# Second-weight operands made in the chunk loop, and M1, M6, M7 summed in one PSUM bank

## The chip, the cores and the metric

The kernel runs on one core of one Trainium2 chip. Times are microseconds on the device. The program is short of nothing but order: five engines work side by side, each through its own queue in the order in which the kernel was written down, TensorE (PE) for matmuls, VectorE (DVE) and ScalarE (ACT) for everything that reads PSUM, GpSimd (POOL) for work between SBUF tiles, SyncE (SP) for issuing DMAs.

## The reference

The input x has 2048 tokens of 576 numbers. With xn the layer norm of x:

```
s = linear_attention(xn, wqkv) @ wo        # 32 heads of 18
h = gelu(xn @ w1 + b1)                     # 576 -> 4608, tanh form
g = silu(h @ w2 + b2)                      # 4608 -> 576
out = x + s * g
```

All of it is in float32. A float32 number is split into a high part that TensorE takes in one pass and a low part, the rest; a product is then three matmuls (high by high, high by low, low by high).

## The kernel before, in words

The program has four stages. First, tokens are normalised and transposed and the keys and values projected, 16 tiles of 128 tokens (the loop over `t`, lines 539 to 640). Second, the queries and the attention output (lines 1069 to 1105). Third, the two dense layers, 18 chunks (lines 1511 to 1607). Fourth, the end of the last chunk with the plain second product and the gate (lines 1608 to 1610).

The chunk loop does the work of the two dense layers with a scheme of seven products in place of eight. A half of the chunks (9) treats 1024 tokens, a chunk 4 of the 36 column tiles of w1 (128 columns each). In a chunk there are two `Up` blocks (j = 0 and 1; class at line 1129), each for a pair of column tiles and two blocks of 512 tokens. An `Up` block computes seven products M1 to M7, each of seven matmuls of 512 columns at line 1147, and from them four outputs, which go through GELU on ACT (line 1155). The order of the seven is written out in `UP` (line 1453). Their sums, with U1 and U2 for partial sums, are:

```
g(0,0) = M1 + M2              U1 = M1 + M6        U2 = U1 + M7
g(1,0) = U1 + M5 + M3         g(1,1) = U2 + M5    g(0,1) = U2 + M4
```

After the two blocks come the seven products of the second layer (`product`, line 1273; order in `ORDER`, line 1269), each in two calls of 24 matmuls in all, added to `macc` by DVE (line 1292). Their moving operands come from the blocks B00, B01, B10, B11 of w2, four of them through differences: operand 5 is B01 - B00, operand 7 is B11 - B01, operand 6 is B11 less operand 5, operand 4 is B10 less operand 6. Each operand is split: its high part by ACT (`set_hi`, line 812), its low part by DVE (`set_lo`, line 815). The stationary operands are the GELU outputs and their sums (class `HOps`; POOL makes the sums at lines 1243 to 1252).

Where the operands of w2 come from differs. In the first half a chunk loads the raw block (line 667), and makes operands 2, 1, 7, 4 and 3 itself, with three subtractions on POOL (lines 1200 and 1205); it stores each to DRAM (line 809) for the second half, which only loads. Operands 5 and 6 were made in the projection stage, for all nine chunks (lines 389 to 423), and stored; both halves load them (line 1223). The operands of w1 are made in the first half's chunks too (class `W1`: four subtractions on POOL at lines 858 to 865, splits at 869 and 874).

PSUM has eight banks here: a pool of two one-bank tiles (`bank1`), from which an `Up` block takes A and E, and a pool of three two-bank tiles (`bank2`), from which it takes two, and every second-layer product one.

What sets the order: a chunk has 28 steps, 7 for each `Up` block and 14 for the half products. At each step the code emits the product, then what the tables have put at that step (`at_step`, line 1495): `P1` and `P0` for w1, `PW2` for w2 (the step of each high part; its low part comes one step later), `PH` for the GELU outputs. The engines run all this strictly in the order in which it was emitted (`in_order`, line 1509), each engine for itself. A matmul that writes a bank waits until the engines that read the bank before are done with it.

```
UP = (1, 6, 7, 5, 2, 3, 4)
PW2 = {2: 0, 1: 1, 7: 3, 4: 5, 3: 8}
ORDER = (1, 2, 7, 4, 5, 3, 6)
```

Of the kernel before, what the change touches and what calls it, by code (L numbers as in the profile page):

```python
# [44 lines left out]
def linear_attention_gated_ffn(ctx, tc, x, xT, wqkv, wo, w1, w1e, b1, w2, b2, out):  # L45
# [90 lines left out]
    w2p = ph1.enter_context(tc.tile_pool(name="w2p", bufs=2, reuse_waits="tile"))  # L136
# [252 lines left out]
    T_OPS = (5, 6)  # L389
    w2raw, w2op = {}, {}  # L390

    def w2_load(c):
        t = w2p.tile([P, 3, 2, HD], F32, tag="w2r", name=f"w2r{c}")
        nc.sync.dma_start(t.rearrange("p b a d -> p (b a d)"), w2[c][:, D:])
        w2raw[c] = t

    def w2_block(c, i):

        B11, B00, B01 = (w2raw[c][:, k] for k in range(3))
        return {5: (B00, B01, B00), 6: (B11, B11, B00)}[i]  # L400

    def w2_sum(j):
        c, i = j // 2, T_OPS[j % 2]
        dst, a, b = w2_block(c, i)
        nc.gpsimd.tensor_tensor(dst, a, b, op=SUB)

    def w2_hi(j):
        shape = [P, 2, 2, HD]
        if j % 4 < 2:
            w2op[j] = stw.tile(shape, F32R, tag="stw", name=f"w2o{j}")  # L410
        else:
            w2op[j] = w2p.tile(shape, F32R, tag="w2o", name=f"w2o{j}")
        nc.scalar.copy(w2op[j][:, 0], w2_block(j // 2, T_OPS[j % 2])[0])

    def w2_lo(j):
        c, i = j // 2, T_OPS[j % 2]
        t = w2op[j]
        nc.vector.tensor_tensor(t[:, 1], w2_block(c, i)[0], t[:, 0].bitcast(F32), op=SUB)

    def w2_store(j):  # L420
        c, i = j // 2, T_OPS[j % 2]
        w2_dram[c, i] = d = dram.tile([P, 2, 2, HD], F32, name=f"op_{c}_{i}")
        nc.sync.dma_start(d, w2op.pop(j).bitcast(F32))

# [33 lines left out]
    W2_AT = (2, 4, 6, 8, 10, 11, 12, 13, 14)  # L458
    W2_LOADS = {0: 0, 1: 1, 3: 2, 5: 3, 7: 4, 9: 5, 11: 6, 12: 7, 13: 8}
    W2_SUMS = {t: (2 * c, 2 * c + 1) for c, t in enumerate(W2_AT)}  # L460

    class XSums:
# [19 lines left out]
        def tt(self, out, a, b, op):  # L482
            nc.vector.tensor_tensor(out, a.bitcast(F32), b.bitcast(F32), op=op)
# [24 lines left out]
        def sum4(self, k):  # L508
            self.tt(self.t, (self.h0, self.l0)[k][:, self.B], self.t, (SUB, ADD)[k])
# [29 lines left out]
    for t in range(NT):  # L539
# [21 lines left out]
        sums2 = W2_SUMS.get(t - 1, ())  # L561
# [17 lines left out]
        if t + 1 < NTR:  # L579
            if t:  # L580
                k_t, _ = phi(t1, pk, f"k{t}", values)
            transpose_x(t + 1)
            if t == 0:
                project(t, wv_h, wv_l, pv, FIRST_V[1], cols=v_cols, begin=False)
            for j in sums2:
                w2_hi(j)
            for j in sums2:
                w2_lo(j)
            if t - 1 in WE_SUMS:
                we_hi(WE_SUMS[t - 1]), we_lo(WE_SUMS[t - 1])  # L590
            if t == 0:
                layernorm(2)
            if t + 2 < NTR:
                offset(t + 2)
            if t == 0:
                k_t, _ = phi(t1, pk, f"k{t}")
        else:
            if not last:
                set_x_hi(t + 1), set_x_lo(t + 1)
            for j in sums2:  # L600
                w2_hi(j)
            for j in sums2:
                w2_lo(j)
# [16 lines left out]
        for j in W2_SUMS.get(t, ()):  # L620
            w2_sum(j)
# [6 lines left out]
        for j in W2_SUMS.get(t - 1, ()):  # L628
            w2_store(j)
# [5 lines left out]
        if t in W2_LOADS:  # L635
            w2_load(W2_LOADS[t])
# [490 lines left out]
    m1_sb, u1_sb, u2_sb = (mid[:, i] for i in range(3))  # L1127

    class Up:


        def __init__(self, n, w, xs):
            self.p, self.w = n % NP, w
            self.xb = xs

            self.a, self.b = bank1(f"a{n}"), bank2(f"b{n}")
            self.zy, self.e = bank2(f"zy{n}"), bank1(f"e{n}")
            self.g = {}
# [19 lines left out]
        def step(self, i):  # L1158
            A, B, E = self.a, self.b[:, 0, :], self.e
            Z, Y = self.zy[:, 0, :], self.zy[:, 1, :]  # L1160
            tt = nc.vector.tensor_tensor
            if i == 1:
                self.mm(A, 1)
                nc.scalar.copy(m1_sb, A)  # L1164
            elif i == 6:
                self.mm(B, 6)
                tt(u1_sb, B, m1_sb, op=ADD)  # L1167
            elif i == 7:
                self.mm(Z, 7)
                tt(u2_sb, Z, u1_sb, op=ADD)  # L1170
            elif i == 5:
                self.mm(E, 5)
                tt(B, E, u2_sb, op=ADD)  # L1173
                self.gelu(1, 1, B)
            elif i == 2:
                self.mm(A, 2, first=False)
                self.gelu(0, 0, A)
            elif i == 3:
                self.mm(E, 3, first=False)
                tt(E, E, u1_sb, op=ADD)  # L1180
                self.gelu(1, 0, E)
            else:
                self.mm(Y, 4)
                tt(Y, Y, u2_sb, op=ADD)
                self.gelu(0, 1, Y)


    class W2:
# [5 lines left out]
        def load_raw(self):  # L1194
            self.raw = raw = load_w2_raw(self.n) if self.n else w2_raw0[0]
            self.B = lambda r, n: raw[:, 2 - 2 * r + n]
            self.src = {1: self.B(0, 0), 2: self.B(1, 0), 3: self.B(1, 1), 7: self.B(0, 1)}

        def sum7(self):
            nc.gpsimd.tensor_tensor(self.src[7], self.src[3], self.src[7], op=SUB)  # L1200

        def sum4(self, k):

            self.src[4] = t = self.src[2]
            nc.gpsimd.tensor_tensor(t, t, self.src[(7, 1)[k]], op=SUB)
# [247 lines left out]
    UP = (1, 6, 7, 5, 2, 3, 4)  # L1453
# [21 lines left out]
    PW2 = {2: 0, 1: 1, 7: 3, 4: 5, 3: 8}  # L1475
    W2_SUMS_NEXT = {5: 23, 6: 27}
    W2_SUMS_FIRST = {5: 6, 6: 10}
# [33 lines left out]
    for step in range(n_chunks):  # L1511
# [19 lines left out]
        if half == 0 and c < NC - 1:  # L1531
# [5 lines left out]
            for i, at in W2_SUMS_NEXT.items():  # L1537
                add(base + at, lambda i=i, n=step + 1: w2t[n].load(i))
# [119 lines left out]
```

## Time and profile before

| | before |
|---|---|
| runs, median of 3 (lowest, highest) | 1097.93 us (1097.7, 1102.11) |
| span of the profiled execution, first to last instruction | 1096.2 us |
| TensorE busy | 1088.2 us, 6702 matmuls |
| VectorE, ScalarE, POOL busy | 829.5, 491.3, 471.5 us |
| mean granted TensorE clock | 0.999 |

The profile is of one execution. Its own time on the device is known only as the span; the runs' median is 1.7 us above it. A row of a group reads: line, engine, operation, output and input tile, shape, count; then busy time and mean ns; then the idle time of the engine in front of it and what ended that. A row of the timeline reads: start in us, duration, engine, line, operation, and in brackets the engine's idle time in front of it. A row of stretches reads: the stretch, its length, the busy time of PE, PE's weight loads, DVE, ACT and POOL (with counts), the granted clock, the DMA engines' busy share and GB/s. The chain's rows are start, duration, engine, tile, line.

### The profile page before, as it was taken

Reading aid. Unit: us, or ns where it says so; the run is one execution under the profiler, and the core shown is the slowest. Engines: PE = TensorE matmul, PEld = TensorE weight load, DVE = VectorE, ACT = ScalarE, POOL = GpSimd, SP = SyncE. Lnnn points to the kernel's source line nnn. Section 1 sums busy time; section 2 is a strip of 40 time slices with the busy share of each in tenths; the row PEclk is TensorE's granted clock in tenths of the full one; section 3 lists DMA queues with packets and bytes.
Section 4 is the critical chain, followed back from the end, with each engine's and each line's share of the span. In section 5 each row is a group of like instructions: output and inputs, shape, how many; then the busy total and the mean of one; then the engine's idle time right before and its main releaser. Section 6 shows DMA issues by size and latency. Waiting matters only on the chain.

```text
span 1096.2 us, 18083 instructions
## 1 busy us (share of the span) xinstructions
PE 1088.2 (99%) x6702; PEld 1008.8 (92%) x6702; DVE 829.5 (76%) x1132; ACT 491.3 (45%) x844; POOL 471.5 (43%) x403
## 2 busy tenths in 40 slices
PE   9999999999999999999999999999999999999998
PEld 8999989999898998989989989899898998989987
DVE  7787748888798888888888888667475584764856
ACT  6555555555545455454453544524234243242442
POOL 3676434323546446464554553424234143242340
PEclk9999999999999999999999999999999999999999
DMA  7898834675959558486585769978676676767452
GB/s 248 264 274 274 309 137 149 206 248 186 333 221 350 182 220 322 160 320 224 189 332 175 284 237 400 391 248 289 215 241 219 210 231 212 238 219 224 126 184 87
DMA packets 88400, 262.54 MB, mean 239 GB/s; under 512 B 11894, under 2 KB 24182, under 8 KB 85624
## 3 DMA queue, kind: packets, MB, share of 16 engines
q1 hardware_dynamic: 88312, 261.38, 69.3%
q8 instruction: 53, 0.87, 0.3%
q14 instruction: 35, 0.29, 0.1%
HBM read 164.24 MB, written 95.17 MB: 237 GB/s over the span
## 4 chain that ended last, share of the span: by engine, by line
PE 99%; DVE 1%; ACT 0%; issue 0%; POOL 0%; DVEq 0%; POOLq 0%
PE pm L1286 35%; PE a L1147 10%; PE e L1147 10%; PE zy L1147 10%; PE pk L321 6%; PE pq L321 5%; PE ps_s L788 5%; PE b L1147 5%; PE pv L321 4%; PE pd L1402 2%; PE ps_kva L382 1%; PE ptp L770 1%; PE ps_kw L707 1%; PE warm L369 0%; DVE wkv_l L364 0%; PE ps_kvb L382 0%
## 5 line engine op out<-in xcount | busy, mean ns | idle before, releaser
L1292 DVE TENSOR_TENSOR macc<-pm,macc 128x576 f32<-128x576 f32 x218 | 163.9, 752 | 49.9 <-PE pm L1286 48.4
L812 ACT CAST h_h<-g 128x512 fp32r<-128x512 f32 x204 | 121.9, 621 | 132.7 <-PE pm L1286 131.5
L815 DVE TENSOR_TENSOR h_l<-g,h_h 128x512 fp32r<-128x512 f32 x204 | 161.8, 800 | 0.0
L1252 POOL TENSOR_TENSOR mid<-g 128x512 f32<-128x512 f32 x34 | 43.9, 1292 | 108.1 <-ACT g L1155 108.1
L1246 POOL TENSOR_TENSOR g<-g 128x512 f32<-128x512 f32 x34 | 54.9, 1616 | 49.5 <-DVE h_l L815 28.4
L1155 ACT ACTIVATE g<-b,b1c 128x512 f32<-128x512 f32 x36 | 24.8, 690 | 102.5 <-DVE b L1173 102.5
L1164 ACT COPY mid<-a 128x512 f32<-128x512 f32 x36 | 21.1, 585 | 95.3 <-PE a L1147 95.3
L858 POOL TENSOR_TENSOR w1raw<-w1raw 128x256 f32<-128x256 f32 x18 | 13.3, 737 | 116.8 <-ACT h_h L812 68.2
L1167 DVE TENSOR_TENSOR mid<-b,mid 128x512 f32<-128x512 f32 x36 | 24.8, 690 | 45.0 <-PE b L1147 41.8
L1374 POOL TENSOR_TENSOR fin1l<-fin1h,fin1l 128x288 f32<-128x288 f32 x8 | 6.5, 811 | 118.4 <-DMA fin1l<-s_dram 69.6
L1249 POOL TENSOR_TENSOR g<-g 128x512 f32<-128x512 f32 x34 | 55.2, 1623 | 2.7
L1147 PE MATMUL a<-h0r,wa 128*128 128x512 f32 x144 | 50.4, 390 | 0.0
L1147 PE MATMUL a<-xh,wa 128*128 128x512 f32 x144 | 50.4, 390 | 0.0
L815 DVE TENSOR_TENSOR h_l<-mid,h_h 128x512 fp32r<-128x512 f32 x34 | 48.8, 1436 | 1.2
L1155 ACT ACTIVATE g<-e,b1c 128x512 f32<-128x512 f32 x36 | 24.8, 690 | 51.9 <-DVE e L1180 51.9
L753 POOL TENSOR_TENSOR pbuf<-phiq,den 128x576 f32<-128x576 f32 x16 | 19.4, 1213 | 63.6 <-DVE den L752 63.6
L1243 POOL TENSOR_TENSOR g<-g 128x512 f32<-128x512 f32 x34 | 44.1, 1296 | 2.7
L1180 DVE TENSOR_TENSOR e<-e,mid 128x512 f32<-128x512 f32 x36 | 24.8, 690 | 22.3 <-PE e L1147 22.3
L1170 DVE TENSOR_TENSOR mid<-zy,mid 128x512 f32<-128x512 f32 x36 | 24.9, 691 | 19.8 <-PE zy L1147 19.8
L1173 DVE TENSOR_TENSOR b<-e,mid 128x512 f32<-128x512 f32 x36 | 25.2, 700 | 18.5 <-PE e L1147 17.4
L321 PE MATMUL pk<-wkv_h,xh 128*128 128x288 f32 (+1 forms) x160 | 38.2, 321 | 0.4 <-ACT xh L248 0.4
L321 PE MATMUL pk<-wkv_l,xh 128*128 128x288 f32 (+1 forms) x160 | 38.4, 321 | 0.0
(857 smaller groups left out, 3646.5 us busy)
## 6 DMA issues: line engine op xcount, KB each, us to landing
we<-we_dram SPq DMA_DIRECT2D x36, 448.0 KB
w2raw<-w SPq DMA_DIRECT2D x10, 1152.0 KB
op<-w2o SPq DMA_DIRECT2D x18, 576.0 KB
w1raw<-w SPq DMA_DIRECT2D x18, 512.0 KB
op_a<-wa SPq DMA_DIRECT2D x18, 512.0 KB
op_c<-wc SPq DMA_DIRECT2D x18, 512.0 KB
op_d<-wd SPq DMA_DIRECT2D x18, 512.0 KB
wc<-op_c SPq DMA_DIRECT2D x18, 512.0 KB
```

The costliest lines, as they stand in the source:

```text
L321: nc.tensor.matmul(ps[:, h, : ws.stop - ws.start], st, w[:, k, ws], start=(begin and i == 0), stop=(end and i == len(seq) - 1), skip_group ...
L788: nc.tensor.matmul(ps[:, h, :HD], st[:, k, :], w[:, k, h * HD : (h + 1) * HD], start=(i == 0), stop=(i == len(seq) - 1),)
L812: nc.scalar.copy(pair[0], src)
L815: eng.tensor_tensor(pair[1], src, pair[0].bitcast(F32), op=SUB)
L1147: nc.tensor.matmul(ps, st, mv, start=first and n == 0, stop=n == len(seq) - 1, skip_group_check=True,)
L1155: nc.scalar.activation(g, ps, AF.Gelu_apprx_tanh, bias=b1c[:, f : f + 1])
L1243: tt(src[5, pr], A(1, 0), A(1, 1), op=ADD)
L1246: tt(src[6, pr], src[5, pr], A(0, 0), op=SUB)
L1249: tt(src[3, pr], A(0, 1), src[6, pr], op=SUB)
L1252: tt(src[7, pr], A(0, 0), A(1, 0), op=SUB)
L1286: nc.tensor.matmul(ps[:, q, :HD], hs[p][st][:, cs], m[:, p, :], start=(n == 0 and i not in CHAIN), stop=(n == 5), skip_group_check=True,)
L1292: nc.vector.tensor_tensor(dst, src, dst, op=ADD)
```

## The change

**The projection stage** no longer makes operands 5 and 6 of w2. Nine loads, 18 subtractions on POOL, 18 splits on ACT and on DVE and 18 stores go, with their tables and the pool `w2p`.

**A chunk of the first half** makes operands 5 and 6 itself. In place of three subtractions on POOL (operand 7 in one, operand 4 in two) it does four, in the order 5, 7, 6, 4, at steps 3 and 4, each overwriting a block of the raw tile. The high and low parts of operands 1, 2 and 3 come ahead of them, those of 7, 4, 5, 6 behind. Operands 5 and 6 are stored like the others, and no longer loaded in the first half. The second half's loads are as before.

**An `Up` block** has the order 1, 2, 6, 5, 7, 3, 4. M1, M6 and M7 are accumulated by TensorE in bank A, one after the other; ACT copies the bank to SBUF after each (M1, then U1, then U2). ACT also copies M5 from E, into the place where M1 was. DVE adds four times (M2 + M1, U2 + M5, M3 + U1, M4 + U2) where it added five times. The two-bank tiles are now `bc`, with M2 in one bank and M4 in the other, and `z`, which only DVE writes (U2 + M5).

```diff
-    T_OPS = (5, 6)
...
-        for j in W2_SUMS.get(t, ()):
-            w2_sum(j)
...
+    m5_sb = m1_sb
...
-            self.a, self.b = bank1(f"a{n}"), bank2(f"b{n}")
-            self.zy, self.e = bank2(f"zy{n}"), bank1(f"e{n}")
+            self.a, self.e = bank1(f"a{n}"), bank1(f"e{n}")
+            self.bc, self.z = bank2(f"bc{n}"), bank2(f"z{n}")
...
+            A, E, Z = self.a, self.e, self.z[:, 0, :]
+            B, C = self.bc[:, 0, :], self.bc[:, 1, :]
             if i == 1:
                 self.mm(A, 1)
                 nc.scalar.copy(m1_sb, A)
+            elif i == 2:
+                self.mm(B, 2)
+                tt(B, B, m1_sb, op=ADD)
+                self.gelu(0, 0, B)
             elif i == 6:
-                self.mm(B, 6)
-                tt(u1_sb, B, m1_sb, op=ADD)
-            elif i == 7:
-                self.mm(Z, 7)
-                tt(u2_sb, Z, u1_sb, op=ADD)
+                self.mm(A, 6, first=False)
+                nc.scalar.copy(u1_sb, A)
             elif i == 5:
                 self.mm(E, 5)
-                tt(B, E, u2_sb, op=ADD)
-                self.gelu(1, 1, B)
-            elif i == 2:
-                self.mm(A, 2, first=False)
-                self.gelu(0, 0, A)
-            elif i == 3:
+                nc.scalar.copy(m5_sb, E)
+            elif i == 7:
+                self.mm(A, 7, first=False)
+                tt(Z, A, m5_sb, op=ADD)
+                nc.scalar.copy(u2_sb, A)
+                self.gelu(1, 1, Z)
+            elif i == 4:
+                self.mm(C, 4)
+                tt(C, C, u2_sb, op=ADD)
+                self.gelu(0, 1, C)
+            else:
                 self.mm(E, 3, first=False)
                 tt(E, E, u1_sb, op=ADD)
                 self.gelu(1, 0, E)
-            else:
-                self.mm(Y, 4)
-                tt(Y, Y, u2_sb, op=ADD)
-                self.gelu(0, 1, Y)
...
+        def T(self, i):
+            src = self.src
+            tt = nc.gpsimd.tensor_tensor
+            B00, B01, B10, B11 = (self.B(r, n) for r in range(2) for n in range(2))
+            dst, a, b = {
+                5: (B00, B01, B00), 7: (B01, B11, B01), 6: (B11, B11, B00), 4: (B10, B10, B11)
+            }[i]
+            tt(dst, a, b, op=SUB)
+            src[i] = dst
...
-    UP = (1, 6, 7, 5, 2, 3, 4)
+    UP = (1, 2, 6, 5, 7, 3, 4)
...
-    PW2 = {2: 0, 1: 1, 7: 3, 4: 5, 3: 8}
+    PW2 = dict(
+        T={5: 3, 7: 3, 6: 4, 4: 4},
+        hi={2: 0, 1: 1, 3: 2, 7: 5, 4: 6, 5: 8, 6: 9},
+        lo={2: 1, 1: 2, 3: 3, 7: 6, 4: 7, 5: 9, 6: 10},
+    )
...
-            add(base, w2t[step].sum7)
-            for k in range(2):
-                add(base + 2, w2t[step].sum4, k)
-            for i, at in PW2.items():
-                add(base + at, w2t[step].hi, i)
-                add(base + at + 1, w2t[step].lo, i)
-            if step == 0:
-                for i, at in W2_SUMS_FIRST.items():
-                    add(at, w2t[0].load, i)
+            for what in ("T", "hi", "lo"):
+                for i, at in PW2[what].items():
+                    add(base + at, getattr(w2t[step], what), i)
...
-            for i, at in W2_SUMS_NEXT.items():
-                add(base + at, lambda i=i, n=step + 1: w2t[n].load(i))
```

More of the change, by code (lines that the diff above doesn't have):

```diff
@@ L135, in linear_attention_gated_ffn @@
     stw = ph1.enter_context(tc.tile_pool(name="stw", bufs=2, reuse_waits="tile"))
-    w2p = ph1.enter_context(tc.tile_pool(name="w2p", bufs=2, reuse_waits="tile"))
     t1 = ph1.enter_context(tc.tile_pool(name="t1", bufs=2, side="right", reuse_waits="tile"))
@@ L385, in state @@
             )
-    T_OPS = (5, 6)
[L390 to L410, printed above, removed]
-        else:
[L412 to L423, printed above, removed]
     we = {}
@@ L457, in linear_attention_gated_ffn @@
     WE_SUMS = {2 * q + 1: q for q in range(WG)}
-    W2_AT = (2, 4, 6, 8, 10, 11, 12, 13, 14)
-    W2_LOADS = {0: 0, 1: 1, 3: 2, 5: 3, 7: 4, 9: 5, 11: 6, 12: 7, 13: 8}
-    W2_SUMS = {t: (2 * c, 2 * c + 1) for c, t in enumerate(W2_AT)}
     class XSums:
@@ L560, in linear_attention_gated_ffn @@
         v_t = v_bufs[t % 2]
-        sums2 = W2_SUMS.get(t - 1, ())
         last = t + 1 == NT
@@ L584, in linear_attention_gated_ffn @@
                 project(t, wv_h, wv_l, pv, FIRST_V[1], cols=v_cols, begin=False)
[L585 to L588, printed above, removed]
             if t - 1 in WE_SUMS:
@@ L599, in linear_attention_gated_ffn @@
                 set_x_hi(t + 1), set_x_lo(t + 1)
[L600 to L603, printed above, removed]
             if t - 1 in WE_SUMS:
@@ L627, in linear_attention_gated_ffn @@
             raw_q[k] = load_w_raw(0, k)
-        for j in W2_SUMS.get(t - 1, ()):
-            w2_store(j)
         if t - 1 in WE_SUMS:
@@ L1196, in load_raw @@
             self.B = lambda r, n: raw[:, 2 - 2 * r + n]
[L1197 to L1205, printed above, removed]
+            self.src = {1: self.B(0, 0), 2: self.B(1, 0), 3: self.B(1, 1)}
+        def T(self, i):
[7 more added lines that the diff above has]
+            src[i] = dst
         def plain(self, f):
```

7 lines of the change are left out of this document (removed).

## The prediction

> **What bounds the kernel now.** I read first the page's busy times and its row of granted clock, then a table of stretches, then the chain that ended last.
>
> ```profile
> span 1096.2 us, 18083 instructions
> PE 1088.2 (99%) x6702; PEld 1008.8 (92%) x6702; DVE 829.5 (76%) x1132; ACT 491.3 (45%) x844; POOL 471.5 (43%) x403
> PEclk9999999999999999999999999999999999999999
> ...
> 0.00:20.00 20.00, 17.39 (x104) 16.31 (x105) 13.52 (x30) 12.59 (x22) 6.90 (x17) 1.00 0.92 326
> 40.00:80.00 40.00, 40.00 (x248) 38.79 (x247) 35.58 (x48) 21.99 (x43) 30.34 (x28) 1.00 1.01 288
> 283.00:685.00 402.00, 402.00 (x2393) 366.80 (x2392) 348.74 (x456) 193.75 (x333) 206.33 (x167) 1.00 0.71 263
> 685.00:1087.00 402.00, 402.00 (x2397) 367.19 (x2396) 259.86 (x349) 139.77 (x225) 130.84 (x101) 1.00 0.67 225
> ```
>
> TensorE sets the end: in both halves of the chunk loop it is busy for 402.00 of 402.00 us, at clock 1.00. The change leaves every matmul in place, so it can gain only where TensorE idles or runs slower. It idles 2.6 us of the first 20, before any product of the chunk loop, and in the tail. For pace I compare chunks in the chain:
>
> ```profile
> 551.47 1.62 PE a L1147 x7
> 553.10 1.60 PE b L1147 x7
> 596.19 1.62 PE a L1147 x7
> ...
> 819.63 1.62 PE a L1147 x7
> 864.29 1.62 PE a L1147 x7
> ```
>
> A chunk takes 44.72 us in the first half and 44.66 in the second, although VectorE works 348.74 us in the one and 259.86 in the other. Taking all of that difference away would give 9 x 0.06 = 0.5 us. With the whole 2.6 us at the start the change can gain at most 3.1 us (0.3%). What is left to ask is whether a matmul has to wait in the new order.
>
> **Work that goes away or moves under cover.** These groups price it:
>
> ```profile
> L405 POOL TENSOR_TENSOR w2r<-w2r 128x576 f32<-128x576 f32 x18 | 28.8, 1598 | 15.6 <-DVE phik L340 8.5 <-DMA w2r<-w 6.4
> L413 ACT CAST w2o<-w2r 128x576 fp32r<-128x576 f32 x18 | 11.5, 672 | 2.5 <-POOL w2r L405 2.5
> L418 DVE TENSOR_TENSOR w2o<-w2r,w2o 128x576 fp32r<-128x576 f32 x18 | 19.1, 1098 | 0.2
> L1164 ACT COPY mid<-a 128x512 f32<-128x512 f32 x36 | 21.1, 585 | 95.3 <-PE a L1147 95.3
> L1167 DVE TENSOR_TENSOR mid<-b,mid 128x512 f32<-128x512 f32 x36 | 24.8, 690 | 45.0 <-PE b L1147 41.8 <-ACT mid L1164 3.2
> op<-w2o SPq DMA_DIRECT2D x18, 576.0 KB
> ```
>
> The projection stage loses 28.8 us of POOL, 11.5 of ACT and 19.1 of VectorE with 9 loads and 18 stores; TensorE is full there (40.00 of 40.00), so that is worth 0. In the chunk loop's first half 18 loads of 576 KB turn into 16 stores at a DMA share of 0.71: 0. On SP's queue the two new stores of a chunk wait for low parts that end, in the walk below, at 19.8 and 20.9, and the next chunk's second load of we stands behind them; its first use is after 44.7, so 0 as well. One VectorE addition fewer in each of 36 Up blocks takes 36 x 0.69 = 25 us from VectorE, three more ScalarE copies give ScalarE 36 x 3 x 0.585 = 63 us. Their sums are covered by 44.7 us of matmuls a chunk; what counts is where each stands in its queue.
>
> **The new waits.** Before, M2 went onto bank A four products after M1, and M3 onto E two after M5. Now M6 goes onto A two products after M1, M7 onto A two after M6, M3 onto E two after M5. Each waits until ScalarE has copied the bank, and one product of cover lies between: 1.6 us, as the row of M6 at 553.10 above has it (1.59 from product to product). The copies stand in ScalarE's queue behind the weight splits, and these behind POOL. So I walk the queues of a first-half chunk. Time 0 is its first matmul, at 551.31.
>
> ```profile
> 551.31 0.40 PE L1147 MATMUL a<-xh,wa 128*128 128x512 f32 x1
> 554.27 0.69 DVE L874 TENSOR_TENSOR wa<-w1raw,wa 128x512 fp32r<-128x512 f32 x1 [1.18 <-ACT wa L869]
> 559.87 1.22 DVE L874 TENSOR_TENSOR wc<-w1raw,wc 128x512 fp32r<-128x512 f32 x1 [0.62 <-ACT wc L869]
> 561.01 1.98 DVE L815 TENSOR_TENSOR w__6302<-w2raw,w__6302 128x576 fp32r<-128x576 f32 x1
> 564.91 0.76 DVE L815 TENSOR_TENSOR w__6336<-w2raw,w__6336 128x576 fp32r<-128x576 f32 x1
> 555.04 0.74 POOL L858 TENSOR_TENSOR w1raw<-w1raw 128x256 f32<-128x256 f32 x1 [4.76 <-DVE wa L874]
> 555.86 1.14 POOL L861 TENSOR_TENSOR w1t<-w1raw 128x256 f32<-128x256 f32 x1
> 556.96 1.32 POOL L863 TENSOR_TENSOR w1raw<-w1raw 128x256 f32<-128x256 f32 x1
> 558.23 0.73 POOL L865 TENSOR_TENSOR w1raw<-w1raw,w1t 128x256 f32<-128x256 f32 x1
> 558.92 3.45 POOL L1205 TENSOR_TENSOR w2raw<-w2raw 128x576 f32<-128x576 f32 x2
> 565.42 0.58 ACT L1164 COPY mid<-a 128x512 f32<-128x512 f32 x1
> 565.60 1.30 POOL L1252 TENSOR_TENSOR mid<-g 128x512 f32<-128x512 f32 x1 [3.22 <-ACT g L1155]
> ```
>
> The reader is to see that VectorE's low parts and POOL's subtractions hold each other up. The low part w__6302 takes 1.98 us beside POOL, its like w__6336 takes 0.76 with POOL idle; it ends 0.62 us after POOL's subtraction ends (562.99 against 562.37). A 256-wide subtraction takes 0.74 or 1.14 to 1.32. Read as turns, one engine after the other, with 0.62 of a 576-wide low part, 0.50 of a 512-wide and 0.28 of a 256-wide inside the turn, and 1.33 and 0.60 of POOL's, the queues of before come out within 0.1 us: the second subtraction ends at 11.04 (562.37 is 11.06), the second block's copy of M1 starts at 14.10 (565.42 is 14.11).
>
> The same walk in the new order. POOL starts after VectorE's low part wa, at 3.65, as now. Its four w1 subtractions end at 7.5. Where two w2 subtractions followed, four do now: T5 ends 9.1, T7 11.1, T6 12.9, T4 14.7, each 1.33 and one low part's turn in between (0.62, 0.50, 0.50, 0.50). ScalarE has done gelu(0,1) of the first block by 14.7 (M4 ends 11.3; its addition on VectorE, behind the low part wd, ends 14.0). Then comes the high part of operand 4, which waits for T4: 14.76 to 15.44. Behind it stands the second block's copy of M1: 15.33 to 15.92, though M1 was done at 12.9. M6 should start at 14.31 and starts at 15.95: **1.64 us** late.
>
> What is late next: the low part of operand 4 is behind POOL's S7 and ends at 17.13; the addition for M2 follows to 17.75, gelu(0,0) 17.78 to 18.47, the high part of operand 5, the copy of M6 18.95 to 19.53. M7, due at 19.13, starts at 19.56: **0.43 us**. M3's wait and the first block's three waits are met, M7's there by only 0.3 us. Products start 2.07 late, and nothing in them is later than that. Nine chunks: 9 x 2.07 = 18.6 us.
>
> Bounds: if no turn were taken, the copy would start at 13.2 and M6 in time: 0. With POOL's turns 0.1 shorter the sum is 1.17 a chunk, with 0.25 longer 4.3. I take 2.07, as the walk fits before's rows within 0.1.
>
> **The tenth chunk** starts with SiLU calls between the GELUs.
>
> ```profile
> 687.78 2.25 ACT L1362 ACTIVATE macc<-macc 128x1152 f32<-128x1152 f32 x2
> 690.74 1.17 ACT L1362 ACTIVATE macc<-macc 128x1152 f32<-128x1152 f32 x1 [0.72 <-DVE macc L1302]
> 691.93 1.28 ACT L1155 ACT_TABLE_LOAD   x1
> 693.23 0.69 ACT L1155 ACTIVATE g<-b,b1c 128x512 f32<-128x512 f32 x1
> ...
> 689.37 0.68 DVE L1167 TENSOR_TENSOR mid<-b,mid 128x512 f32<-128x512 f32 x1
> ```
>
> Today the first gelu follows all three SiLUs. Now gelu(0,0) stands before the third: SiLUs to 690.03, a table load (1.30 with its gap), gelu to 692.0, a load, SiLU to 694.4, then the copy of M6 to 694.9. M7 is due 6.37 after this chunk's start (685.66), at 692.03: 2.9 us once. Bounds 0 (were the third SiLU ready first) and 2.9.
>
> [...]
>
> In the second half there are no weight splits in ScalarE's queue; a copy starts 0.03 us after its matmul and lasts 0.585, well within 1.59: 0.
>
> **Sum.** Span 1096.2 + 18.6 + 2.9 = 1117.7. The median of the runs, 1097.93, lies 1.7 above the profiled span, so **1119.4 us**, 2.0% slower.
>
> **Rivals.**
> *Not slower.* POOL keeps ahead: its subtractions run unheld, four of 0.74 and four of 1.44 from 3.65, and T4 ends at 12.4, ahead of gelu(0,1); the copy of M1 is then in time. For it: four 256-wide ones do run at 0.73 to 0.74. Against: L861's 1.14 and L1205's 3.45. It decides as soon as T4 ends before 13.0. Only the tenth chunk is left: 1097.9 + 2.9 = 1100.8, or 1098 without it.
> *Bank reuse becomes the wait.* C now shares a tile with B and is read last, by gelu(0,1). If the second pm tile takes that buffer, its matmuls wait for addition and gelu.
>
> ```profile
> 841.89 22.40 PE pm L1286 x168
> 842.39 0.69 DVE L1184 TENSOR_TENSOR zy<-zy,mid 128x512 f32<-128x512 f32 x1
> ```
>
> The addition ends 843.08, a gelu of 0.69 would end 843.8; the second pm tile is due one product after 841.89, at 843.49: 0.3 a chunk, some 0.6 in the first half, where VectorE is a third busier. 17 chunks: 9 x 0.6 + 8 x 0.3 = 7.8 (the 0.6 is an estimate, twice the 0.3), so 1105.7 by itself, 1127 on top. Against: the tile of Z is free three products earlier, and I take the pool to give out the buffer that was free first.
> *Worse.* Turns are longer with eight subtractions in a row: 4.3 x 9 + 2.9 = 41.6, so 1139.5. Against: the turns of before are 0.1 exact.
> *Faster.* The 3.1 us at most come and nothing waits: 1095, which the clock of 1.00 and the full stretches leave no more room for.
>
> **How the numbers follow.** Forecast 0.70 (its own range, 1.0 to 3.0 a chunk, 1109 to 1128); not slower 0.10; bank reuse 0.10; worse 0.08; faster 0.02. No change means within 0.5%, 5.5 us, about what a measurement of this kernel can tell. Slower 0.88, same 0.10, faster 0.02. From 1104 to 1130 it holds the forecast and the bank rival, 0.80.
>
> **What would show it.** Right: PE with idle time at L1147's M6 and M7, ended by ACT's copy, once a chunk in the first half and only in its second block; ACT waiting for POOL before operand 4's high part; chunks of about 46.8 us in the first half and 44.66 in the second, the tenth 47.6; two table loads more than now. Wrong: chunks of 44.72; or waits at pm; or idle time in the first block or all over the second half.

## The result, and the profile after

The changed kernel takes 1129.0 us (median of 4 runs, 1128.05 to 1129.45), 1.027 times the kernel before on the same chip, 95% interval [1.0247, 1.0292]; four runs of the kernel before there lie between 1097.7 and 1102.11 us, median 1099.92. The forecast was 1119.4, range 1104 to 1130. The direction and the place were right, the size was too small: 21.5 us were forecast, and 29.1 were measured over the median of four, 31.1 over the 1097.93 from which the forecast was reckoned.

The page of the changed kernel, its span and busy times:

```profile
span 1126.3 us, 18080 instructions
PE 1098.3 (98%) x6702; PEld 1012.0 (90%) x6702; DVE 774.1 (69%) x1096; ACT 551.5 (49%) x954; POOL 461.9 (41%) x394
```

VectorE has 55 us less to do and ScalarE 60 more. TensorE has the same 6702 matmuls and is busy 10 us longer, because some of them run slower, and by its rows it waits 20.5 us besides. The waits, longest first (total us, times, longest):

```profile
PE a L1090 <- ACT mid L1107: 17.5, 9, 2.1
PE a L1090 <- ACT mid L1114: 3.0, 1, 3.0
```

Line 1107 is ScalarE's copy of M1, line 1114 that of M1 + M6. The first stall comes nine times, once in each first-half chunk, the second once, in the tenth. Two stretches, each as long as one first-half chunk and begun some 0.2 us behind its first matmul:

```profile
377.22:424.44 47.22, 45.17 (x268) 40.73 (x267) 38.71 (x51) 25.59 (x45) 26.42 (x20) 1.00 0.63 233
424.44:473.01 48.57, 46.54 (x267) 41.87 (x267) 37.81 (x51) 25.78 (x45) 26.40 (x20) 0.96 0.60 226
```

Six of the nine chunks take about 47.22 us (44.72 before), three 48.57 to 48.61. What sets the three apart is the granted clock, 0.96 instead of 1.00; with the same work TensorE is busy 1.37 us longer in the second row. Second-half chunks take 44.65, as before. Here is the stall in the timeline, first with the full clock (chunk from 377.06), last the M6 of the next chunk:

```profile
377.06 0.40 PE L1090 MATMUL a<-xh,wa 128*128 128x512 f32 x1
...
384.20 1.29 DVE L757 TENSOR_TENSOR w__4251<-w2raw,w__4251 128x576 fp32r<-128x576 f32 x1
384.84 7.52 POOL L1151 TENSOR_TENSOR w2raw<-w2raw 128x576 f32<-128x576 f32 x4
...
386.02 1.32 DVE L816 TENSOR_TENSOR wc<-w1raw,wc 128x512 fp32r<-128x512 f32 x1
387.86 1.32 DVE L816 TENSOR_TENSOR wd<-w1raw,wd 128x512 fp32r<-128x512 f32 x1
389.71 1.38 DVE L757 TENSOR_TENSOR w__4307<-w2raw,w__4307 128x576 fp32r<-128x576 f32 x1
391.16 0.39 PE L1090 MATMUL bc<-xh,we 128*128 128x512 f32 x1
392.39 0.67 ACT L754 CAST w__4319<-w2raw 128x576 fp32r<-128x576 f32 x1 [1.87 <-POOL w2raw L1151]
392.97 0.58 ACT L1107 COPY mid<-a 128x512 f32<-128x512 f32 x1
393.60 1.65 PE L1090 MATMUL a<-s,w 128*128 128x512 f32 x6 [2.05 <-ACT mid L1107]
395.99 0.59 ACT L1114 COPY mid<-a 128x512 f32<-128x512 f32 x1
396.92 0.39 PE L1090 MATMUL a<-xh,wc 128*128 128x512 f32 x1
...
440.80 2.80 PE L1090 MATMUL a<-s,w 128*128 128x512 f32 x6 [2.03 <-ACT mid L1107]
```

It reads as the prediction had it: the four subtractions on POOL take turns with four low parts on VectorE; ScalarE idles 1.87 us for the last of them (operand 4), makes its high part, and only then copies M1, which M6 waits for. After the same gap M6's six matmuls take 1.65 us in one chunk and 2.80 in the next: that is the dip of the clock.

The tenth chunk, ScalarE and then TensorE:

```profile
713.99 2.25 ACT L1309 ACTIVATE macc<-macc 128x1152 f32<-128x1152 f32 x2
716.26 1.28 ACT L1098 ACT_TABLE_LOAD   x1
717.55 0.69 ACT L1098 ACTIVATE g<-bc,b1c 128x512 f32<-128x512 f32 x1
718.26 1.28 ACT L1309 ACT_TABLE_LOAD   x1
719.55 1.16 ACT L1309 ACTIVATE macc<-macc 128x1152 f32<-128x1152 f32 x1
720.62 0.57 ACT L1114 COPY mid<-a 128x512 f32<-128x512 f32 x1
721.24 0.80 PE L1090 MATMUL a<-h1r,wc 128*128 128x512 f32 x1 [3.00 <-ACT mid L1114]
```

The GELU stands between the second and the third SiLU, two table loads come with it, and M7 waits 3.0 us.

The difference of the two spans, 30.1 us, from the first matmuls of the chunks: nine first-half chunks 26.6 more, the tenth 4.67 (49.34 against 44.67), the start, the rest of the second half and the tail together 1.1 less.

### The profile page after: what moved, and what is told of

It is laid out like the page before. It is cut to its first block, busy times and chain, and to the rows that moved or that the text cites. A ratio compares the mean times of both kernels' runs of the same rounds, so it can differ in the third digit from the quotient of the medians.

```text
span 1126.3 us, 18080 instructions
## 1 busy us (share of the span) xinstructions
PE 1098.3 (98%) x6702; PEld 1012.0 (90%) x6702; DVE 774.1 (69%) x1096; ACT 551.5 (49%) x954; POOL 461.9 (41%) x394
## 4 chain that ended last, share of the span: by engine, by line
PE 87%; POOL 5%; issue 2%; ACT 2%; DVE 2%; DMA 1%; SPq 0%; POOLq 0%; ACTq 0%; DVEq 0%
PE pm L1233 34%; PE a L1090 12%; PE e L1090 8%; PE bc L1090 6%; PE pk L320 6%; PE pq L320 5%; PE ps_s L730 5%; PE pv L320 4%; POOL w2raw L1151 4%; PE pd L1349 2%; PE ps_kva L381 1%; DMA op_c<-wc 1%; PE ptp L712 1%; POOL w1t L803 1%; DMA b2b<-b 1%
## 5 line engine op out<-in xcount | busy, mean ns | idle before, releaser
L757 DVE TENSOR_TENSOR h_l<-g,h_h 128x512 fp32r<-128x512 f32 x204 | 157.9, 778 | 11.8 <-ACT h_h L754 11.5
L1098 ACT ACTIVATE g<-bc,b1c 128x512 f32<-128x512 f32 x72 | 49.6, 689 | 55.9 <-DVE bc L1110 39.3
L1107 ACT COPY mid<-a 128x512 f32<-128x512 f32 x36 | 21.1, 585 | 95.2 <-PE a L1090 94.0
L1151 POOL TENSOR_TENSOR w2raw<-w2raw 128x576 f32<-128x576 f32 x36 | 65.2, 1810 | 2.1
L1120 DVE TENSOR_TENSOR z<-a,mid 128x512 f32<-128x512 f32 x36 | 25.0, 695 | 51.0 <-PE a L1090 51.0
L1110 DVE TENSOR_TENSOR bc<-bc,mid 128x512 f32<-128x512 f32 x36 | 25.0, 694 | 41.7 <-PE bc L1090 39.8
L1090 PE MATMUL a<-s,w 128*128 128x512 f32 x108 | 32.1, 438 | 17.5 <-ACT mid L1107 17.5
L1121 ACT COPY mid<-a 128x512 f32<-128x512 f32 x36 | 21.1, 587 | 50.0 <-DVE z L1120 50.0
L1090 PEld LDWEIGHTS a<-s,w 128*128 128x128 f32 x108 | 21.6, 207 | 25.6 <-ACT mid L1107 21.3
L339 DVE SCALAR_TENSOR_TENSOR phik<-pk,ek 128x576 f32<-128x576 f32 x16 | 12.1, 758 | 37.0 <-ACT ek L337 37.0
L730 PE MATMUL ps_s<-kw_h,th 128*128 128x288 f32 x160 | 35.5, 303 | 0.0
```

The source lines that it names most:

```text
L730: nc.tensor.matmul(ps[:, h, :HD], st[:, k, :], w[:, k, h * HD : (h + 1) * HD], start=(i == 0), stop=(i == len(seq) - 1),)
L757: eng.tensor_tensor(pair[1], src, pair[0].bitcast(F32), op=SUB)
L1090: nc.tensor.matmul(ps, st, mv, start=first and n == 0, stop=n == len(seq) - 1, skip_group_check=True,)
L1098: nc.scalar.activation(g, ps, AF.Gelu_apprx_tanh, bias=b1c[:, f : f + 1])
L1151: tt(dst, a, b, op=SUB)
```

## The experiments

The twelve were timed beside the kernel before, whose medians there were 1097.2 to 1097.7; the row of the changed kernel is the result above. "Chunk" is a usual first-half chunk, from first matmul to first matmul.

| | time, us | ratio to before, 95% | chunk, us | TensorE waits for, in the first-half chunks |
|---|---|---|---|---|
| before | 1097.4 | 1 | 44.72 | nothing |
| changed | 1129.0 | 1.027 [1.0247, 1.0292] | 47.22, 48.57 | copy of M1 |
| 1 new Up alone | 1106.6 | 1.0080 [1.0065, 1.0095] | 45.18 | copy of M1, a little |
| 2 operands alone | 1116.1 | 1.0171 [1.0156, 1.0186] | 46.86 | VectorE: M3, products |
| 3 operand 4 split later | 1119.7 | 1.0208 [1.0191, 1.0225] | 46.79 | VectorE: products |
| 4 operands 4, 5, 6 later | 1125.8 | 1.0256 [1.0239, 1.0274] | 47.60 | VectorE: products |
| 5 one low part later | 1119.3 | 1.0196 [1.0181, 1.0211] | 46.60 | copy of M1 |
| 6 one subtraction more | 1156.0 | 1.0529 [1.0513, 1.0545] | 51.1 | copy of M1 |
| 7 spread | 1109.4 | 1.0106 [1.0091, 1.0121] | 45.52 | VectorE: products |
| 8 spread, SiLUs later | 1106.0 | 1.0076 [1.0059, 1.0093] | 45.51 | VectorE: products |
| 9 fill, operand 4 at 11 | 1112.8 | 1.0137 [1.012, 1.0154] | 46.28 | VectorE, ScalarE: products |
| 10 fill, operand 4 at 13 | 1110.3 | 1.0114 [1.0099, 1.0129] | 45.98 | VectorE: products; copy of M1 |
| 11 low parts later still | 1105.9 | 1.0081 [1.0068, 1.0095] | 45.50 | VectorE: low part of 4 |
| 12 low parts on GpSimd | 1102.05 | 1.0041 [1.0028, 1.0055] | 45.11 | two of 0.2, products |

**1 and 2: each part alone.** The first keeps the old operands and takes the new `Up`; the second takes the operands and keeps the old `Up` with its order.

```diff
 # run 1, in the kernel before, with the new Up
-    UP = (1, 6, 7, 5, 2, 3, 4)
+    UP = (1, 2, 6, 5, 7, 3, 4)
 # run 2, in the changed kernel, with the old Up
-    UP = (1, 2, 6, 5, 7, 3, 4)
+    UP = (1, 6, 7, 5, 2, 3, 4)
```

> The Up block alone is changed (order 1, 2, 6, 5, 7, 3, 4 and the sums in bank A); operands 5 and 6 are made in the projection stage as before. Theory (the wait is ScalarE's copy of M1 behind operand 4's high part behind POOL): POOL has two w2 subtractions left in a chunk, the last ends at 11.1 of the chunk, so M6 is late only by some 0.4 us in the second block through the longer queue, 9 x 0.4 plus 9 x 0.27 for the restart = 6, and the tenth chunk keeps its loss of 4.7: about 1109 to 1111, ratio 1.010. Rival (the one product of cover is too short by itself, whatever stands ahead of the copy): the waits of 2 us stay, 1.027. Rival (all of it comes from making the operands in the chunk): only the tenth chunk, 1.004.

> The operands alone are moved into the chunk; the Up block is the one of before. Theory: operand 4's high part still waits for POOL and the copy of M1 still ends at 16.0 of the chunk, but M2 goes onto the bank only four products after M1, so that wait is gone; the additions behind the copy on VectorE are late and M3 may wait 0.7 us in the second block: 9 x (0.7 + 0.27) = 9 us at most, nothing in the tenth chunk, 1098 to 1107, ratio 1.000 to 1.008. Rival (the load on POOL and VectorE itself costs the time): as much as both together, 1.02 or more.

Waits of the first, then of the second:

```profile
PE a L1148 <- ACT mid L1172: 3.0, 1, 3.0
...
PE a L1148 <- ACT mid L1165: 1.9, 8, 0.2
```

```profile
PE e L1089 <- DVE b L1115: 6.1, 9, 0.7
PE pm L1230 <- DVE h_l L757: 4.3, 9, 0.5
...
PE pm L1230 <- DVE macc L1236: 1.9, 7, 0.3
```

The new `Up` costs 9.2 us: 1106.6 is below the 1109 to 1111 expected and above the rival with the tenth chunk alone (ratio 1.004). Over half of it is in that chunk (49.57 us against 44.67). The operands alone cost 18.7, far more than expected, and hardly through ScalarE (one wait of 0.3 us): with the old `Up`, M3 and the second layer's products wait for VectorE. The two sum to 27.9, and the changed kernel has 29.1 over its own runs of before, 31.6 over the ones here. So the larger part is the operands, whichever engine's instruction TensorE is seen to wait for.

**3 and 4: take the late high part out of ScalarE's way.** The first moves only operand 4's split behind the second block, the second those of 5 and 6 as well, and the tenth chunk's SiLUs to step 13.

```diff
 # run 3
+        hi={2: 0, 1: 1, 3: 2, 7: 5, 5: 8, 6: 9, 4: 14},
+        lo={2: 1, 1: 2, 3: 3, 7: 6, 5: 9, 6: 10, 4: 15},
 # run 4
+        hi={2: 0, 1: 1, 3: 2, 7: 5, 4: 14, 5: 14, 6: 15},
+        lo={2: 1, 1: 2, 3: 3, 7: 6, 4: 15, 5: 15, 6: 16},
+            for m in (C22, C21, C12):
+                add(base + 13, silu_first, m)
```

> The whole change, with the high and low part of operand 4 moved from steps 6 and 7 to steps 14 and 15, behind the second Up block. Theory: the copy of M1 no longer stands behind POOL's last subtraction, M6 is on time, no clock dips in the first half; what is left is the tenth chunk's 4.7 us and at most 9 x 0.4 at the first half product: 1103 to 1106, ratio 1.004 to 1.007. Rival (cover too short, or ScalarE has too many copies): waits at M6 or M7 stay in the first half's chunks and the ratio stays above 1.015.

> As the run before, with operands 5 and 6 also split behind the second Up block (steps 14 to 16) and the tenth chunk's three SiLU calls put behind its second Up block (step 13) instead of between its first GELUs. Theory: no product waits anywhere, chunks of 44.7 us throughout, the tenth included; 1097 to 1099, ratio 0.998 to 1.001. Rival (the tenth chunk's loss has another cause than the table loads and the third SiLU ahead of the copy): 4.7 us stay, ratio 1.004.

Both missed. The waits of the first, and VectorE's timeline in its chunk that starts at 516.27:

```profile
PE pm L1233 <- DVE macc L1239: 7.4, 8, 0.9
PE pm L1233 <- DVE h_l L757: 3.2, 8, 0.4
```

```profile
542.89 1.82 DVE L757 TENSOR_TENSOR w__5915<-w2raw,w__5915 128x576 fp32r<-128x576 f32 x1
544.63 1.78 DVE L757 TENSOR_TENSOR h_l<-mid,h_h 128x512 fp32r<-128x512 f32 x1
546.33 0.74 DVE L1239 TENSOR_TENSOR macc<-pm,macc 128x576 f32<-128x576 f32 x1
...
549.29 0.75 DVE L1239 TENSOR_TENSOR macc<-pm,macc 128x576 f32<-128x576 f32 x1
...
550.18 0.50 PE L1233 MATMUL pm<-w__5915,h_h 128*128 128x288 f32 x2 [0.91 <-DVE macc L1239]
```

M6's wait went (one of 0.5 us is left, in one chunk), and nearly as much came back in the products: operand 4's low part takes 1.82 us beside GpSimd's sums, the hidden operand's low part behind it 1.78, and the additions that free the PSUM tiles stand behind both. So ScalarE's copy was not the only bound: with its wait gone, VectorE's queue is the next, and the chunk is only 0.43 us shorter (46.79 against 47.22). The second, with three splits there, stalls more (1.3 and 1.2 at the longest), which fits the same cause with a larger dose.

**5 and 6: one turn less, one subtraction more.** If turns between VectorE and GpSimd set M6, one low part less between the subtractions must give about half a microsecond, and one more subtraction must take its time; and a longer gap may tell what the dips of the clock hang on. Run 5 moves the low part of operand 4 by a step too, so that it stays behind that of operand 7; run 6 does its extra subtraction in the nine first-half chunks.

```diff
 # run 5
+        lo={2: 1, 1: 2, 3: 3, 7: 8, 4: 8, 5: 9, 6: 10},
 # run 6, in W2.T
+            if i == 4:
+                flat = lambda v: v.rearrange("p a d -> p (a d)")[:, :512]
+                tt(mid[:, 3], flat(a), flat(b), op=SUB)
```

> The changed kernel with one step moved: the low part of the first half's operand 7 (VectorE) at step 8 instead of step 6 of the chunk, so that VectorE and GpSimd have one turn fewer to take before the subtraction that makes operand 4. Turn-taking theory: each 576-wide low part taken out from between the four subtractions lets the last of them end 0.5 us earlier, so M6 of the second block waits about 1.8 us instead of 2.2 to 2.3: 9 x 0.5 = 4.4 us less, 1124.5 us; if the shorter wait also spares the dips of the granted clock (3 x 1.4 us) 1120.5. Rival, VectorE's queue as a whole is full through the second block and the first products: the low part only comes later in the same queue, and TensorE's wait moves to the products: 1127 to 1131 us.

> The changed kernel with one more GpSimd subtraction (128 x 512, result unused) just before the subtraction that makes operand 4, in each of the ten chunks of the first half. It takes 0.7 us alone and about 1.3 with VectorE's turns between, so M6 of the second block should wait about 3.5 us instead of 2.2 in nine chunks: +9 x 1.3 = 11.7 us. Theory that the granted clock dips after a long enough gap in TensorE's work: the dip, seen in 3 of 9 chunks after gaps of about 2 us, comes in nearly all nine, + up to 6 x 1.4 = 8 us more: 1141 to 1149 us, nearer the upper, with the low granted clock behind nearly each of the gaps. Rival, the dip has nothing to do with the gap's length: again in about three chunks, 1141 us. Rival, the ScalarE queue and not GpSimd sets M6: 1129 us.

The wait, and the stretch of all nine first-half chunks, of the first:

```profile
PE a L1090 <- ACT mid L1107: 14.4, 9, 1.7
```

```profile
282.80:702.10 419.30, 404.79 (x2397) 366.28 (x2395) 340.83 (x455) 233.11 (x405) 228.28 (x177) 1.00 0.66 251
```

The wait fell from 2.05 to 1.6 us, every chunk takes 46.5 to 46.6, and the clock is 1.00 through all nine: no dip. 9.7 us less, 9 x 0.6 from the chunks' length and 4.1 from the dips, a little more than forecast. Of the second, the wait, the stretches of the first and the fourth chunk, and one M6 in the timeline:

```profile
PE a L1090 <- ACT mid L1107: 30.2, 9, 3.4
```

```profile
282.01:331.57 49.56, 46.57 (x269) 41.67 (x268) 37.59 (x49) 27.50 (x47) 27.57 (x21) 0.97 0.65 247
...
432.56:483.67 51.11, 47.70 (x269) 42.68 (x268) 38.08 (x51) 25.84 (x45) 27.37 (x21) 0.93 0.57 215
```

```profile
450.46 2.93 PE L1090 MATMUL a<-s,w 128*128 128x512 f32 x6 [3.41 <-ACT mid L1107]
```

The gap grew by 1.36 us. The 1.3 expected came out, though not by the way it was reckoned (0.7 us alone and a turn): the same four low parts stand beside the subtractions, so no turn was added, and a GpSimd subtraction of this size takes 1.29 us, not 0.7 (median of line 1199 in the changed kernel). The clock is now below 1.00 in all nine chunks, 0.97 in two and 0.93 in seven. So the dips depend on the gap; the last section shows how. A dip also costs more after the longer gap: 51.1 less 44.72, less 3.41 of idle time, less 0.45 that goes with each gap (47.22 less 44.72 less 2.05), leaves 2.5 us, where the changed kernel's slow chunks lose 1.36 (48.58 less 47.22). So the time, 1156, lies above what either theory expected.

**7 and 8: the same work, spread.** The subtractions for operands 6 and 4 between GpSimd's two groups of sums, the splits of 4, 5, 6 just ahead of their use; the second also has the SiLUs at step 13.

```diff
+        T={5: 3, 7: 3, 6: 12, 4: 12},
+        hi={2: 0, 1: 1, 3: 2, 7: 5, 4: 16, 5: 17, 6: 18},
+        lo={2: 1, 1: 2, 3: 3, 7: 6, 4: 17, 5: 18, 6: 19},
```

> The changed kernel with the same work at other steps of the chunk: the two subtractions for operands 6 and 4 at step 12 (between GpSimd's sums of the two pairs), the high and low parts of operands 4, 5, 6 at steps 16 to 19, one or two steps ahead of their use, where GpSimd is idle in the trace before. Theory that the cost is where the exclusive turns of VectorE and GpSimd lie (all four subtractions beside six low parts ahead of the second block's M6): the second-operand half of the cost goes, what stays is that of the new Up alone (1106.6 us): 1105 to 1110 us. Rival, VectorE (87% busy in a chunk before) has no room for two more low parts anywhere, and TensorE waits for it in the products, by about 2 us a chunk as in the run with the operands alone: 1118 to 1126 us.

> As the spread kernel, and in the tenth chunk the three SiLUs of the finished blocks at step 13, behind the second block's GELUs, instead of steps 0 and 1. Theory: the tenth chunk's wait of 3.0 us for the copy behind the SiLUs, with its restart and the dip of the clock behind it (4.7 us in all), goes: 1101 to 1105 us, 4 to 5 less than the spread kernel. Rival, the SiLUs' table loads hold up the high parts of the hidden operands at step 13 on, so that TensorE waits in the tenth chunk's products instead: within 2 us of the spread kernel.

The first is in the range of the theory. The second saves another 3.4 us, less than the 4 to 5 expected, and 1106.0 is above its range of 1101 to 1105, because the tenth chunk's products now have two small waits (46.1 us). Nothing of the change's work is left out, and run 8 is 23 us faster than the changed kernel. What remains in its chunks is 0.79 us each, and its timeline shows where:

```profile
495.11 1.18 DVE L757 TENSOR_TENSOR w__5450<-w2raw,w__5450 128x576 fp32r<-128x576 f32 x1
496.21 0.68 DVE L757 TENSOR_TENSOR h_l<-g,h_h 128x512 fp32r<-128x512 f32 x1
496.81 0.75 DVE L1239 TENSOR_TENSOR macc<-pm,macc 128x576 f32<-128x576 f32 x1
...
497.70 0.50 PE L1233 MATMUL pm<-w__5450,h_h 128*128 128x288 f32 x2 [0.36 <-DVE macc L1239]
```

The first product of operand 4 needs the addition of product 7, and that stands behind operand 4's own low part.

**9, 10 and 11: other places on VectorE.** In all three the SiLUs are at step 13.

```diff
 # run 9
+        T={5: 3, 7: 3, 6: 9, 4: 9},
+        hi={2: 0, 1: 1, 3: 2, 7: 5, 5: 6, 4: 11, 6: 20},
+        lo={2: 1, 1: 2, 3: 3, 7: 6, 5: 7, 4: 12, 6: 21},
 # run 10, T as in run 9
+        hi={2: 0, 1: 1, 3: 2, 7: 5, 5: 6, 4: 13, 6: 20},
+        lo={2: 1, 1: 2, 3: 3, 7: 6, 5: 7, 4: 14, 6: 21},
 # run 11, T as in runs 7 and 8
+        hi={2: 0, 1: 1, 3: 2, 7: 5, 4: 16, 5: 18, 6: 20},
+        lo={2: 1, 1: 2, 3: 3, 7: 6, 4: 18, 5: 20, 6: 21},
```

> As the spread kernel with the SiLUs at step 13, with the added work where the trace of that kernel shows VectorE and GpSimd idle: operand 5 split at steps 6 and 7 (VectorE idle 1.2 us there), the subtractions for operands 6 and 4 at step 9, operand 4 split at steps 11 and 12, operand 6 at steps 20 and 21. In the spread kernel a first-half chunk takes 45.51 us against 44.72 before: TensorE waits 0.4 us for VectorE's addition of product 7, which stands behind operand 4's low part (1.18 us) at step 17. Theory of turns and places: without that low part in the products the wait goes, nine chunks come back to between 44.7 and 45.1 us: 1099 to 1102 us, level with the kernel before. Rival: VectorE is full through the second block's end too, so that the low part at step 12 makes the GELUs or the hidden operands late and TensorE waits in the first products: 1104 to 1108 us.

> As the kernel before it in this call, with operand 4 split at steps 13 and 14 instead of 11 and 12, behind the second block's last GELU. Theory: the low part then stands ahead of the first additions of the products, where VectorE has 0.6 us idle: 1099 to 1103 us. Rival: it takes 1.2 us with GpSimd's turns and makes the additions of product 1 late, for which product 2 waits: 1104 to 1108 us. If both kernels come out within 2 us of the spread kernel with the SiLUs moved (1106), VectorE has no place for the work that costs nothing.

> As the spread kernel with the SiLUs at step 13 (1106.0 us), with the low parts of operands 4, 5, 6 at steps 18, 20, 21 instead of 17, 18, 19 (high parts of 5 and 6 at 18 and 20). In the spread kernel VectorE's addition of product 7, first pair, waits behind operand 4's low part (1.18 us, between GpSimd's sums) and a hidden operand's low part (0.68), and the first product of operand 4 waits for it: that stall and a second, smaller one after it are what is left of 0.79 us a chunk. Theory: with operand 4's low part one step later the addition is 1.2 us earlier and both stalls go: nine chunks at 44.7 to 44.9 us, 1098 to 1101 us, level with the kernel before within its uncertainty or up to 0.3% above. Rival: product 4 then waits for the low part itself, or product 5 for its own: 1103 to 1106 us.

All three missed: the first two are 6.8 and 4.3 us slower than run 8, slower than their rivals had it too, and the third is level with it, as its rival had it. The idle spots on VectorE at which they aimed were not free. In run 10, two of the stalls (TensorE's weight loads first, then a matmul):

```profile
481.91 1.23 PEld L1090 LDWEIGHTS a<-s,w 128*128 128x128 f32 x6 [0.49 <-ACT mid L1107]
...
495.18 0.53 PE L1233 MATMUL pm<-w__5199,h_h 128*128 128x288 f32 x2 [0.26 <-DVE macc L1239]
```

M6 waits for the copy of M1 again (the high part of operand 5 is now ahead of it in ScalarE's queue), and product 2 for the addition of product 1. In run 11 the addition of product 7 comes earlier as meant, by 0.65 us of the chunk's time, and the first product of operand 4 waits for the low part instead. Why it did not help is in one stretch of its chunk, 16.3 us from the second addition of product 1 on:

```profile
490.49:506.81 16.32, 16.17 (x118) 15.55 (x117) 16.32 (x23) 7.39 (x14) 6.41 (x6) 1.00 0.42 147
```

The fourth figure is VectorE's: 16.32 busy of 16.32. Inside a full queue the order only chooses who waits.

**12: three low parts on the engine that is idle there.** GpSimd makes the low parts of operands 4, 5 and 6.

```diff
+            set_lo(self.ops[i], self.src[i], nc.gpsimd if i in (4, 5, 6) else nc.vector)
...
+        T={5: 3, 7: 3, 6: 12, 4: 12},
+        hi={2: 0, 1: 1, 3: 2, 7: 5, 4: 13, 5: 17, 6: 18},
+        lo={2: 1, 1: 2, 3: 3, 7: 6, 4: 14, 5: 18, 6: 19},
```

> As the spread kernel with the SiLUs at step 13, with the low parts of operands 4, 5 and 6 made by GpSimd instead of VectorE, at steps 14, 18 and 19 (high part of 4 at step 13). In the run before this one VectorE works without a pause for 15 us of the products (from 490.5 to 506.8 us), while GpSimd stands idle for 9.7 us of the same stretch, and 0.78 us a chunk were left. Theory that VectorE's queue through the products is the last bound: three low parts of 0.74 us each out of it leave 2.2 us of slack a chunk, nine chunks come back to 44.7 to 44.9 us, 1098 to 1101 us, level with the kernel before (1097.2) within 0.4%. Rival, the turns that the low parts take on GpSimd hold up the hidden operands' low parts as much as they did on VectorE: 1104 to 1107 us.

```profile
495.58 1.90 POOL L757 TENSOR_TENSOR w__5472<-w2raw,w__5472 128x576 fp32r<-128x576 f32 x1
...
503.17 0.74 POOL L800 TENSOR_TENSOR w1raw<-w1raw 128x256 f32<-128x256 f32 x1 [3.82 <-ACT h_h L754]
```

1102.05 us, a chunk of 45.11, half of the remaining 0.79 gone: between the two theories, nearer the first, just above the range of 1098 to 1101. A low part takes 1.90 us on GpSimd beside VectorE's work, against 0.74 on VectorE by itself (run 11), and it fits because GpSimd has room there (3.82 us idle in front of the last row). This is the fastest form of the change that was run; it is still 0.4% slower than the kernel before, 0.39 us x 9 of it in the nine chunks and 1.4 in the tenth. No run beat the kernel before.

## Why the prediction was right, and where it was not

**What bounds the kernel** held. TensorE was full before, so no work taken from VectorE or the projection stage could give more than 3.1 us; start, second half and tail gave 1.1.

**The walk of the queues** named the right chain: the subtraction for operand 4, its high part, the copy of M1, M6 of the second block. Its times were near: copy of M1 from 15.33 predicted, 15.91 in the trace (392.97 less 377.06); M6 at 15.95, in the trace 16.54. M6 was due at 14.33 (one matmul of 0.227 us behind the one at 391.16) and came 2.21 late, not 1.64. The step that was mis-sized is the end of the fourth subtraction, 14.7 predicted, 15.3 measured: the four start 0.28 later, and they take 7.52 us instead of 7.2. Four times 1.33 and four whole turns (0.62, 0.50, 0.50, 0.62) make 7.56. The walk put the last turn at 0.50 and let the first overlap in part: with its own turns whole it would have come to 7.44, not 7.2.

**The second wait**, 0.43 us at M7, did not come. The copy of M6 ended where it was predicted (19.53; 396.58 less 377.06 is 19.52), but M6 itself was later than in the walk, and M7, started at 19.86, found the copy done. The two terms together were 2.07, the trace has 2.21. That this is so near is partly luck: the first term is 0.57 too small, and the second, 0.43, did not come.

**What the sum left out.** A chunk without a dip is 2.50 longer, not 2.21: by the matmuls' starts, 0.14 is in M6's first ones behind the gap and 0.15 at operand 4's product. And 3 x 1.36 us in chunks whose clock dipped. So nine chunks: 9 x 2.50 + 3 x 1.36 = 26.6 where 18.6 stood. The clock, 1.00 throughout before, was taken as given; that a wait of TensorE can cost two thirds of its length on top (1.36 on 2.05 us here) was nowhere in the sum. The nine chunks, 2.95 longer on average, are still within the 1.0 to 3.0 that the forecast's own range allowed, but that room was made for longer turns and not for the clock, and 1129.0 is 1 us above the end of that range, 1128, and 1 us below the end of the whole one. That it is inside is partly luck too.

**The tenth chunk**: the wait is 3.0, predicted 2.9, with the two table loads as walked. It costs 4.67, since the clock dips there too (0.50 from 720.86 to 724.27). A switch between SiLU and GELU costs the load of 1.28 us here and hardly more: the GELU starts 1.29 us after the load does (716.26 and 717.55), and the load 0.02 us after the SiLU in front of it ends.

**The rivals.** Bank reuse: no matmul of a product waits for a GELU, and the second half is unchanged. POOL ahead: ruled out, ScalarE idles 1.87 us for it. Worse: 4.3 a chunk was too much, against 2.95 measured. But the closest thing to a missed rival is that the copy of M1 was one of several bounds within half a microsecond of each other: the prediction priced what the copy's lateness costs and did not say that without it VectorE's queue would cost nearly as much, as runs 2, 3 and 4 show.

## What to carry to other kernels

When work is moved out of a stage with a full TensorE into another one, ask which of the stage's helpers is full there, not on average: VectorE was 87% busy over the first half before, and in run 11 100% for 16 us of a chunk; runs 3, 4, 9, 10 and 11 mostly moved the stall, and run 12, which gave the work to an idle engine, halved what was left. A wait removed at the head of a full queue moves down the queue; test that by taking away the load, not only by shifting the instruction that is waited for. And put a wait of a full TensorE down at more than its length: here a chunk with 2.05 us of it took 2.5 longer, or 3.9 where the clock dipped.

## What the runs showed of the hardware

**The granted clock fell after short gaps, where enough of a gap lay in one window.** In first-half chunks with one gap each: 1.6 us, 0 of 9 chunks below 1.00 (run 5); 2.05 us, 3 of 9 (changed kernel); 3.4 us, 9 of 9 (run 6). Between kernels the tenth chunk's gap of 3.0 us gave a dip in the changed kernel (0.86 from 716 to 728) and in run 1 (0.86 from 692 to 704), and none in run 3 (1.00 from 703.4 to 751.4), where that chunk took 47.98 us instead of the changed kernel's 49.34. So the length of the gap alone does not decide. Narrow stretches show what does. In the chunk loop of the changed kernel's trace the clock stands at 0.50 in four stretches of 3.41 us, from 440.96, 536.54, 679.90 and 720.86. These starts are 28, 42 and 12 times 3.413 us apart, so in this trace they lie on one grid of windows of 3.413 us. The rows are two windows with a gap of 2.03 us inside the first, then two that share a gap of 2.05 (1.62 and 0.43), then the two that share the gap of 3.0 in run 3 and the one behind them (the second figure is TensorE's busy time, the one behind POOL's the clock):

```profile
437.55:440.96 3.41, 1.38 (x7) 0.84 (x6) 1.41 (x2) 1.54 (x4) 3.25 (x4) 1.00 0.85 244
440.96:444.38 3.42, 3.42 (x9) 2.68 (x10) 1.80 (x3) 1.86 (x4) 1.57 (x1) 0.50 1.02 384
...
389.76:393.17 3.41, 1.79 (x8) 1.13 (x7) 1.41 (x3) 1.47 (x3) 3.33 (x3) 1.00 0.87 222
393.17:396.59 3.42, 2.99 (x13) 2.48 (x14) 2.10 (x3) 2.64 (x6) 2.11 (x2) 1.00 1.02 414
...
707.98:711.40 3.42, 1.98 (x9) 1.31 (x7) 0.66 (x2) 3.38 (x4) 0.00 (x0) 1.00 0.97 319
711.40:714.81 3.41, 1.85 (x8) 1.53 (x9) 0.00 (x0) 2.00 (x3) 0.00 (x0) 1.00 0.94 324
714.81:718.22 3.41, 3.41 (x17) 2.81 (x16) 1.46 (x3) 2.49 (x4) 0.00 (x0) 1.00 1.00 323
```

Idle for 2.03 us of a window, TensorE has half the clock in the next; a gap of 3.0 us that two windows share, 1.4 and 1.6, leaves it at 1.00. On the changed kernel's grid, from 20 us to 8 us before the end, the four windows with 1.98, 2.03, 2.05 and 2.61 us idle are each followed by one at 0.50; the others at full clock have at most 1.77 us idle, and none of them is. That agrees with 0 of 9, 3 of 9 and 9 of 9: 1.6 us is too little, 2.05 is enough only if nearly all of it falls into one window, and of 3.4 more can fall there. In run 6's fourth chunk the clock is 0.81 from 447 to 451 us, 0.50 to 455 and 0.84 to 459, which makes 6.8 us at 0.50, two windows, from 449.5 to 456.3. Of its gap of 3.41 us, which ends at 450.46, 2.4 lie in the window ahead of these two and 1.0 in the first of them. Two such windows in 51.1 us are the 0.93 that it shares with six other chunks.

**Turns between VectorE and GpSimd could be added up here.** Four subtractions beside four low parts took 7.52 us; the sum of single turns is 7.56. By the rows each holds up the other: a 576-wide low part took 1.29 and 1.38 us beside the subtractions, 0.76 before with GpSimd idle, and a subtraction 1.88 on average, a single one before 1.44 (median of line 1200). But in the walk that fits them only 0.62 of a low part's 0.75 us counts against the other engine, so a sum over whole instructions (four of 1.44 and 0.75, 0.68, 0.68, 0.75 make 8.6) would have come out too long.
